# Half chunks in the first group, wide clock products, and a reordered end in a cross-network kernel

## The chip, the cores and the metric

The kernel runs on one core of a Trainium2 chip. The metric is the device time of the core in microseconds (us); lower is better. A run with 5 rounds gives five or six timed executions, set against executions of the kernel before on the same chip.

## The reference

Six layers of a cross network on 16,384 rows of 416 features, in bfloat16:

```python
B, F, D, L = 16384, 26, 16, 6          # Din = F * D = 416
def reference(x0, ws, bs):
    x = x0
    for l in range(6):
        proj = jnp.einsum('bd,de->be', x, ws[l]) + bs[l]
        x = x0 * proj + x
    return x
```

The kernel keeps x transposed (features on partitions) and cuts 416 features into three full tiles of 128 and a tail of 32. The rows are eight groups of 2048, each of four chunks of 512. Groups are worked in pairs, layer by layer: TensorE (PE) multiplies, ScalarE (ACT) adds the bias, VectorE (DVE) does `x0 * proj + x`. Group 0 is loaded in natural order and transposed by PE. All later groups are loaded by transposing DMAs. The last layer of the last group writes natural-order output directly, for which x itself (the "residual") must be transposed back by DMA.

## The kernel before

Loads, in the order of the SP queue:

```python
    def load_group(g, between=lambda: None):
        ...
        turn(0)                          # a transposing DMA: 2048 rows x 128 features
        add("sp", lambda h: h.dma_start_transpose(Tb, x0[rows, D - P:D]), ...)   # the tails
        turn(1)
        turn(2)
        between()
        for j in range(NJ):              # four small copies of the tails, after Tb has landed
            q = slice(j * T32, (j + 1) * T32)
            add("sp", lambda h, q=q, j=j: h.dma_start(x0s[s][q, XW:XW + CH], Tb[P - T32:P, j * CH:(j + 1) * CH]), ...)
    ...
    load_nat(0, 0, 2)
    load_nat(0, 2, KK)
    load_wm(0, "sp")
    for j in range(1, NJ):
        load_nat(j, 0, KK)               # chunks 1 to 3 of group 0, each whole
    load_w3(0, "sp")
    load_group(1, lambda: load_wm(1, "sp"))
```

The products that only keep the clock up ("clock products"), and the first job:

```python
    def keep_busy(n, b):
        for _ in range(n):
            add("pe", lambda h: h.matmul(bank(b, n=P), ones[:, :], ones[:, :], start=True, stop=True), ...)
    keep_busy(22, 7)

    def transposed_chunk(j):             # 16 transposes: tiles 0, 1, 2 and a fourth that holds the 32 tails
        first = (0, P, 2 * P, D - P)
        ...                              # then two ACT copies, a DVE copy, and a 32-row DVE copy of the tails

    def first_job():
        transposed_chunk(0)
        ...
        keep_busy(8, 3)
        full(g, l, 0, ba, True, True, chunks=[0])
        full(g, l, 1, bb, True, True, chunks=[0])
        transposed_chunk(1)
        transposed_chunk(2)
        full(g, l, 0, ba, True, True, chunks=[1])
        transposed_chunk(3)
        load_w3(1, "act")
        full(g, l, 1, bb, True, True, chunks=[1])
        full(g, l, 0, ba, True, True, chunks=[2, 3])
        ...
```

The end:

```python
    def rest_turn(t):                    # the residual, one transposing DMA per tile
        add("sp", lambda h: h.dma_start_transpose(
            x5f[:, :, t * P:(t + 1) * P], xs[s][:, t * GC:(t + 1) * GC]), ...)
    ...
    spread("act")                        # tails of group 6 into its output tile
    store(LAST - 1, 0, 2)                # group 6: two halves of 832 KB
    store(LAST - 1, 2, NJ)
    ...                                  # row block 0 of the last job
    for j in (0, 2):
        nat_mul(0, j)
        sums.append((0, j))
    nat_sum()                            # one sum; the other is carried into the next row block
    for kk in range(1, KK):
        ...                              # each block: two products and two sums, one sum late throughout
```

## Time and profile before

| | |
|---|---|
| time, three runs at the outset | 476.79 us (476.71 to 477.15) |
| span of the profiled execution | 475.7 us |
| first tail product of group 1 | 22.78 us |
| first product of the last job | 458.39 us |
| last PE product, last DVE sum, end of span | 470.78, 472.89, 475.69 us |

The three last rows are the marks to cut a trace into head, middle and end. The change touches nothing between the second and the third.

The first line covers 8 to 24 us (0.4 us a slice), the second 460 to 464 us (0.1 us a slice). The third is the page's own line on the queue that fetches instructions.

```profile
GB/s 256 126 103 130 23 20 180 291 290 224 108 152 102 10 164 289 287 308 219 206 215 251 249 292 179 243 288 289 288 228 264 354 175 119 67 18 0 0 0 146
GB/s 46 0 0 15 138 202 218 218 200 215 205 369 223 205 200 156 38 3 0 0 0 8 8 8 10 10 8 10 13 207 289 289 292 292 287 294 292 287 323 377
q8 instruction: 26, 0.43, 0.4%
```

A transposing load runs at 287 to 294 GB/s, and now and then nearly everything stops: near 10 and near 13.2 us in the first line, from about 461.7 to 462.9 in the second. The last two of these stops each follow the start of one instruction fetch of 16 KB (0.43 MB in 26 packets on that queue), which ran from 12.05 to 13.01 and from 461.19 to 462.14 us; near the stop at 10 us there is none.

### The profile page before, as it was taken

What the parts mean: (1) busy time and instruction counts of PE and PEld (TensorE: products, weight loads), DVE (VectorE), ACT (ScalarE), POOL (GpSimd) and SP (SyncE); (2) the same over time, 40 slices, a digit from 0 to 9 for tenths busy, and PEclk for the clock granted to TensorE, in tenths of its full rate; (3) what the DMA queues carried; (4) which work ended last, traced back from release to release, by engine and by line L of the source; (5) the groups of instructions that cost most, each with busy time, mean ns of one, the idle gap of its engine ahead of it and who ended that gap; (6) DMA issues with size and microseconds to landing.
All of it is one profiled execution on the core that took longest, in us unless ns stands there. A gap on an engine that the chain in (4) does not pass through costs nothing.

```text
span 475.7 us, 8355 instructions
## 1 busy us (share of the span) xinstructions
PE 462.2 (97%) x3325; PEld 195.7 (41%) x3379; DVE 404.0 (85%) x696; ACT 342.4 (72%) x372; POOL 6.8 (1%) x15
## 2 busy tenths in 40 slices
PE   7999999999999999999999999999999999999995
PEld 6344444444444444444444444434444444444442
DVE  2888888888888888898889869988888888888896
ACT  4677777777777777777777777777777777777785
POOL 1000000000000000000000000000000000000000
PEclk9999999999999999999999999999999999999999
DMA  8866950640002397369308940990000039025899
GB/s 223 181 150 137 190 113 1 142 81 1 28 7 44 63 228 158 76 139 244 84 21 195 208 108 9 178 279 2 1 10 25 4 64 242 15 45 117 227 155 288
DMA packets 138363, 53.31 MB, mean 112 GB/s; under 512 B 112330, under 2 KB 137428, under 8 KB 138324
## 3 DMA queue, kind: packets, MB, share of 16 engines
q1 hardware_dynamic: 137848, 52.46, 49.2%
q8 instruction: 26, 0.43, 0.4%
q10 hardware_dynamic: 476, 0.32, 0.2%
q14 instruction: 13, 0.11, 0.1%
HBM read 5.97 MB, written 13.63 MB: 41 GB/s over the span
## 4 chain that ended last, share of the span: by engine, by line
PE 95%; issue 1%; DMA 1%; ACT 1%; DVE 1%; SPq 0%
PE ps L456 77%; PE ps L477 7%; PE ps L497 6%; PE ps L798 2%; DMA x<-in_x_dram 1%; PE ps L471 1%; ACT tw L394 1%; PE ps L561 1%; PE ps L488 1%; DVE x L864 0%; PE ps L809 0%; ACT x L852 0%; DVE x L858 0%; PE ps L841 0%; SPq L521 0%
## 5 line engine op out<-in xcount | busy, mean ns | idle before, releaser
L394 ACT ACTIVATE tw<-ps,bias 128x1024 bf16<-128x1024 f32 (+1 forms) x295 | 299.8, 1071 | 119.8 <-PE ps L477 80.7
L456 PE MATMUL ps<-x,wm 128*128 128x512 bf16 x1638 | 371.7, 379 | 5.8 <-issue 3.7
L456 PEld LDWEIGHTS ps<-x,wm 128*128 128x128 bf16 x1692 | 158.9, 98 | 213.5 <-issue 27.9
L403 DVE TENSOR_TENSOR tw<-tw,x 128x1024 bf16<-128x1024 bf16 (+1 forms) x285 | 192.3, 682 | 52.8 <-ACT tw L394 52.4
L408 DVE TENSOR_TENSOR x<-tw,x 128x1024 bf16<-128x1024 bf16 (+1 forms) x285 | 183.0, 682 | 0.0
L477 PE MATMUL ps<-x,w 32*128 32x512 bf16 x512 | 39.2, 379 | 0.0
L497 PE MATMUL ps<-x,wm 128*32 128x512 bf16 x564 | 33.0, 380 | 0.0
L434 ACT ACTIVATE ts<-ps,bias 128x512 bf16<-128x512 f32 x47 | 28.8, 701 | 0.0
L438 DVE TENSOR_TENSOR x<-ts,x 128x512 bf16<-128x512 bf16 x47 | 18.6, 417 | 3.7 <-DMA x<-x 3.6
L497 PEld LDWEIGHTS ps<-x,wm 128*32 128x32 bf16 x564 | 13.8, 96 | 17.6 <-issue 5.3
L477 PEld LDWEIGHTS ps<-x,w 32*128 32x128 bf16 x512 | 7.8, 92 | 27.6 <-issue 27.1
L436 DVE TENSOR_TENSOR ts<-ts,x 128x512 bf16<-128x512 bf16 x47 | 18.5, 417 | 0.0
L666 POOL COPY ost<-ot 128x512 bf16<-128x512 bf16 x6 | 5.4, 898 | 423.7 <-DMA ot<-x 423.7
L798 PE MATMUL ps<-wm,x 128*128 128x416 bf16 x48 | 9.5, 340 | 0.0
L852 ACT ACTIVATE x<-ps 128x416 bf16<-128x416 f32 x16 | 7.7, 533 | 2.0 <-PE ps L798 1.9
L568 DVE COPY x<-ps 128x512 bf16<-128x512 bf16 x4 | 1.7, 424 | 8.7 <-PE ps L561 8.7
L565 ACT ACTIVATE x<-ps 128x512 bf16<-128x512 bf16 x8 | 4.3, 594 | 5.6 <-PE ps L561 5.6
L798 PEld LDWEIGHTS ps<-wm,x 128*128 128x128 bf16 x48 | 4.3, 98 | 4.2 <-issue 1.0
L561 PE MATMUL ps<-ident,x 128*128 128x128 bf16 x64 | 4.6, 226 | 1.4 <-DMA x<-in_x_dram 0.9
L858 DVE TENSOR_TENSOR x<-x,x 128x832 bf16<-128x832 bf16 (+1 forms) x10 | 5.0, 504 | 1.1 <-ACT x L852 1.1
L488 PE MATMUL ps<-x,w 32*32 32x512 bf16 x188 | 5.9, 374 | 0.0
L471 PE MATMUL ps<-x,w 32*32 32x512 bf16 x208 | 5.6, 385 | 0.0
(38 smaller groups left out, 35.7 us busy)
## 6 DMA issues: line engine op xcount, KB each, us to landing
out_dram<-ost SPq DMA_DIRECT2D x6, 1664.0 KB, 7.1
x<-in_x_dram SPq DMA_DIRECT2D x7, 416.0 KB, 8.0
x<-x SPq DMA_DIRECT2D x24, 96.0 KB, 2.2
wm<-in_ws_dram SPq DMA_DIRECT2D x6, 312.0 KB, 3.7
out_dram<-ost SPq DMA_DIRECT2D x2, 832.0 KB, 6.7
x<-x SPq DMA_DIRECT2D x22, 64.0 KB, 2.0
out_dram<-x SPq DMA_DIRECT2D x3, 416.0 KB, 3.6
x<-ost SPq DMA_DIRECT2D x28, 32.0 KB, 2.2
```

Of the source, the lines that this page charges most:

```text
L394: add("act", lambda h, a=a, w=w, b0=b0: h.activation(tw[r][:, a * CH:(a + w) * CH], psum[:, b0 * CH:(b0 + w) * CH], ACT_F.Identity, bias=b ...
L403: add("dve", lambda h, a=a, e=e: h.tensor_tensor(tw[r][:, a * CH:e * CH], tw[r][:, a * CH:e * CH], x0s[s0][:, i * GC + a * CH:i * GC + e * ...
L408: add("dve", lambda h, a=a, e=e: h.tensor_tensor(xs[so][:, i * GC + a * CH:i * GC + e * CH], tw[r][:, a * CH:e * CH], src(i, a, e), ALU.ad ...
L434: add("act", lambda h: h.activation(ts[r][:, :], bank(b), ACT_F.Identity, bias=bias[:, 3, l:l + 1], scale=1.0), reads=[("ps", b), "bias"], ...
L436: add("dve", lambda h: h.tensor_tensor(ts[r][:, :], ts[r][:, :], x03, ALU.mult), reads=[("ts", r)] + tok0, writes=[("ts", r)], release=True)
L438: add("dve", lambda h: h.tensor_tensor(x3s[so][:, :], ts[r][:, :], res, ALU.add), reads=[("ts", r)] + rtok, writes=[("x3", so), ("x3", so, ...
L456: add("pe", lambda h, t=t, j=j: h.matmul(bank(banks[j]), wm[l][:, t, ecols], src(t, j, j + 1), start=(first and t == 0), stop=(not first a ...
L471: add("pe", lambda h, q=q, j=j, r=r, c=c, o=o: h.matmul(psum[o, banks[j] * CH:(banks[j] + 1) * CH], w3[l][q, i * P + c * T32:i * P + (c + ...
L477: add("pe", lambda h, q=q, j=j, r=r: h.matmul(bank(banks[j]), w3[l][q, ecols], src[q, :], start=first, stop=not first, tile_position=(r * ...
L488: add("pe", lambda h, l=l, b=b, s3=s3, ri=ri, qi=qi, ro=ro, qo=qo: h.matmul(psum[qo, b * CH:(b + 1) * CH], w3[l][qi, NT * P:D], s3[qi, :], ...
L497: add("pe", lambda h, t=t, j=j, src=src, l=l, b=b, ro=ro, qo=qo: h.matmul(psum[qo, b * CH:(b + 1) * CH], wm[l][:, t, NT * P:D], src(t, j, ...
L798: add("pe", lambda h, t=t: h.matmul(bank(b, n=D), xcol(t, j, kk), wm[l][:, t, :], start=(first and t == 0), stop=(not first and t == NT - 1)),
```

## The change

It has five intents: PE is to begin on half chunks and transpose all 32-wide tails of group 0 together, in four column groups at once; the second weights are to give way to group 1's tail copies; the clock products are to need fewer instructions; the spread, a quarter store and a halved residual are to use DMA earlier at the end; and the sums are to run without their lag, the last store in two. Cut to its core:

```diff
-    def load_group(g, between=lambda: None):
+    def load_group(g):
         turn(1)
         turn(2)
-        between()
         for j in range(NJ):
             ...                                        # tail copies
+        if g == 1:
+            load_wm(1, "sp")
+            load_w3(1, "sp")
     for j in range(1, NJ):
-        load_nat(j, 0, KK)
+        load_nat(j, 0, 2)
+        load_nat(j, 2, KK)
     def keep_busy(n, b):
-        for _ in range(n):
-            add("pe", lambda h: h.matmul(bank(b, n=P), ones, ones, ...))
+        while n > 0:
+            m = min(n, 4)                               # one product of 512 columns for four of 128
+            add("pe", lambda h, m=m: h.matmul(bank(b, n=m * P)..., ones, ones....broadcast_to([P, m, P]), ...))
+            n -= m
     def transposed_chunk(j):
-        ...                                            # 16 transposes, chunk by chunk
+        for k2 in (0, 2):                              # 12 transposes, half by half
+            ...
+    def transposed_tails(b):                           # 16 transposes 32 wide, 4 column groups; one DVE copy
-        keep_busy(8, 3)
+        keep_busy(5, 3)
         full(g, l, 0, ba, True, True, chunks=[1])
+        full(g, l, 1, bb, True, True, chunks=[1])
         transposed_chunk(3)
-        load_w3(1, "act")
-        full(g, l, 1, bb, True, True, chunks=[1])
+        transposed_tails(7)
     def rest_turn(t):
-        add("sp", ... whole tile ...)
+        for j0, j1 in ((0, NJ),) if t == 0 else ((0, 2), (2, NJ)):
+            if t and j0:
+                store(LAST - 1, 0, 1)                   # a quarter, 416 KB, between the halves
+            add("sp", ... chunks j0 to j1 ...)
         if (g, l) == (LAST, L - 2) and i < NT - 1:
+            if i:
+                spread("act")
             rest_turn(i)
-    spread("act")
-    store(LAST - 1, 0, 2)
+    store(LAST - 1, 1, 2)
     store(LAST - 1, 2, NJ)
-    ...                                                # sums one behind
+    ...                                                # sums at once; last block: store of chunks 0-1, then 2, then 3
```

## The prediction

> **What bounds the kernel now.** I read the page first: busy time, then the chain that ended last.
>
> ```profile
> PE 462.2 (97%) x3325; PEld 195.7 (41%) x3379; DVE 404.0 (85%) x696; ACT 342.4 (72%) x372; POOL 6.8 (1%) x15
> ...
> PE 95%; issue 1%; DMA 1%; ACT 1%; DVE 1%; SPq 0%
> ```
>
> TensorE (PE) is busy 97% of 475.7 us and is 95% of the chain. The change touches none of the products between about 25 and 455 us, so it can only win (a) the us by which PE reaches its unbroken stretch earlier, (b) gaps at the hand-over to the last job, (c) what follows PE's last product. I therefore read the chain in order of time at both ends. Columns: start, duration, what.
>
> ```profile
> 2.13 5.75 DMA x<-in_x_dram
> 7.88 0.05 issue
> 7.92 1.08 PE ps L561 x16
> 9.01 0.02 issue
> 9.03 0.43 DVE x L568
> 9.46 0.10 issue
> 9.56 1.05 PE ps L561 x16
> 10.61 0.65 PE ps L456 x3
> 11.26 0.89 PE ps L561 x16
> 12.15 0.05 issue
> 12.21 1.89 PE ps L456 x8
> ```
>
> Chunk 1 of the first group lands at 7.88, PE transposes it (L561), waits for a copy, transposes chunk 2, and so on; the last products of chunks 1 to 3 end at 14.10. From there PE runs without a real gap. The chain names the copy at L568 before chunk 2, but the landing records of the trace have chunk 2 landing at 9.42, nearly together with that copy's end (9.45): both held it. Of chunk 1, 15 of 16 landing parts were there by 6.51 and the last at 7.88; for chunk 2 it is 7.55 and 9.42. One lagging part decides.
>
> The end, same columns, then three lines of the timeline (start, duration, engine, line, count, idle before it):
>
> ```profile
> 470.31 0.38 DVE x L858
> 470.69 1.01 DVE x L864 x2
> 471.69 0.58 DVE x L858 x2
> 472.27 0.02 issue
> 472.30 0.59 DVE x L864
> ```
> ```profile
> 454.98 4.59 ACT L394 ACTIVATE tw<-ps,bias 128x512 bf16<-128x512 f32 x7 [0.21 <-PE ps L456]
> ...
> 459.41 0.67 ACT L664 ACTIVATE ost<-ot 128x512 bf16<-128x512 bf16 x1
> ...
> 459.97 0.27 PE L827 MATMUL ps<-ident,x 32*128 32x32 bf16 x16
> ...
> 464.49 0.59 DVE L864 TENSOR_TENSOR x<-x,x 128x832 bf16<-128x832 bf16 x1 [0.32 <-DMA x<-x]
> ```
>
> VectorE (DVE) has two sums back to back at 470.69: one is a sum held over from the row block before (the lag). ScalarE (ACT) is gapless from 454.98 to 460.08; the spread of group 6's tails (L664) is its last piece. The last store is issued at 472.92 and lands at 475.2.
>
> **What the Trainium skill says.** (1) "DMA: Bandwidth & Descriptors", section "Why a DMA increments its semaphore by 16 and not by 1": only the full 16 means that all data has landed. The trace agrees: the 7.88 above is the 16th part. Halving a load does not remove a lagging part, it only lets half the data be counted earlier. (2) Same page, "Queues, rings and completion order": each DMA engine consumes descriptors in ring order. So what is put ahead on the SP queue delays what is behind; the second transposed half will queue behind the quarter store. (3) "TensorE: Matmul & The Clock Gate", Part 3: small products in different 32-column groups run concurrently. The trace agrees on the 32-wide tail products: 12 of L497 took 0.76 us of the chain, where 12 full ones take 2.7. (4) Same page, Part 1: the clock is released by some 3.4 us of activity, not by a count. Here transposes go from 105 to 56 ns apart at about 4.0 us, 3.0 us after the first product.
>
> **The change part by part.**
>
> *Wide clock products.* 22 products of 128 columns took 2.53 us (0.115 each, slow clock). 6 wide ones stream the same 2816 columns: about the same time. Later 2 become 1 of the same columns, and 8 become 5 columns' worth of 128. They lie ahead of data that PE waits for (PE idles 0.87 us before 7.92). Worth 0.
>
> *Half chunks, and tails apart.* Each of four chunks loses its 4 fourth-column transposes: 16 at 56 ns is 0.9 us of PE, of which the 12 in chunks 1 to 3 (0.67) lie on the path. Added are 16 narrow ones in 4 concurrent column groups, about 4 x 0.06 to 0.3 us, and one 128x512 copy (0.42 on DVE) in place of four 32-row copies (0.43 each). Reckoned forward: chunk 2's second half lands at about 9.45 (same bytes, same lagging part; its first half was transposed before, in the time in which PE now waits). Six transposes: 9.85. Six products of chunk 1 at 0.216: 11.15. Chunk 3, 12 transposes: 11.82. Tails: 12.15. Six products of chunks 2 and 3: 13.45, plus about 0.1 because bank 7 is read by the tail copy first. Before: 14.10. Gain 0.55, say **0.6**.
>
> *Does the next group follow?* The SP queue gets three more load issues of 0.43, so 1.3 us later for the transposing loads of group 1. But their first one sat in issue from 6.44 to 10.56, because transposing packets stood still until the lagging part was through at 10.4; most of the 1.3 falls into that. Second weights now come behind the tail copies and off the ACT queue.
>
> ```profile
> 18.02 0.59 SPq L280 DMA_DIRECT2D wm<-in_ws_dram x1
> ...
> 18.66 2.52 SPq L304 DMA_DIRECT2D x<-ost x4
> ...
> 22.77 0.12 PEld L477 LDWEIGHTS ps<-x,w 32*128 32x128 bf16 x8 [0.42 <-DMA x<-ost]
> ```
>
> The four tail copies landed at 22.53, just ahead of their use at 22.78. Moving the 0.6 us weight issue behind them lets them land near 21.9 plus any delay of the transposes; the earlier PE wants them at 22.1 to 22.2. That fits with up to 0.2 of delay: this reordering is what lets the 0.6 through. The second weights then are issued near 20.5 and land 3.1 to 3.8 later, about 24.3; they are wanted at 25.9 less 0.6. Also hidden. I take 0.1 off: head **-0.5**.
>
> *Spread before the last tile's evictions.* The spread's source landed at 457.16, and ACT ends the tile before at 457.25: no wait, but the 0.67 us now stands ahead of the last four evictions, which end at 460.24 instead of 459.56. The tail transposes (L827, at 459.97) need those banks, so they move to about 460.3, and the copy behind them (L834) and PE's next transposes (460.97) with it. Cost **+0.3**, less if PE has other slack.
>
> *Quarter store between transposed halves.* The residual's first half can be issued at 458.7 (its tile is done at 458.58, SP free at 458.73) instead of 459.21. The quarter store, 416 KB at the 330 to 375 GB/s that this stretch shows, puts 1.2 us ahead of the second half, which then lands near 464.4, as now. DMA idles from 461.5 to 463 in the trace, so stores start about 1.5 us sooner, but none of them ends the program. Worth 0 by itself; it lets sums start without the lag.
>
> *Sums unlagged, last store split.* After the last ACT piece (471.33) DVE still has, before: two products and one wide sum, ending at 472.89. After: without the held-over wide sum, product 1 ends 470.69, sum 0-1 471.24, products 2 and 3 471.9, two narrow sums at about 0.34 each: 472.55. Gain 0.34. The last stores carry 104 KB instead of 208 KB: at 350 GB/s 0.3 us less, of which I count half. Together **-0.5**.
>
> Sum: -0.5 + 0.3 - 0.5 = -0.7; with the head's uncertainty leaning to a gain I take -0.8: 476.79 - 0.8 = **476.0 us**.
>
> **Rivals.** *Group 1 becomes the wait.* If the three extra issues delay the transposed loads by the full 1.3 us, tail copies land at 23.2 and PE waits 1.1 us: the head loses 0.4 instead of gaining, and the time is near 477. For: the copies now land only 0.25 us ahead. Against: the stand-still up to 10.4, and the weights taken out of the way. *The lagging part moves.* It may not lag with twice as many, smaller packets; then chunk 2 lands near 7.6 and the head gains until group 1 binds, 0.9 us at most: 475.5. *The residual's second half lands late* (behind the store, after 465.3): DVE has only 0.3 us of slack for each row block of 2.67 us, so unlagged sums would carry the delay to the end and eat the 0.34: 476.4. *The spread costs nothing* if L827's place has more slack than I see: 475.7.
>
> **Range and chances.** The parts are each under 1 us and 2% is 9.5 us, so only a failure outside this list leaves the band. Runs of the kernel before spread over 0.44 us. The rivals span 475.5 to 477; 8 in 10 from 475.2 to 476.8. Faster by over 2%: 0.01; within 2%: 0.98; slower: 0.01.
>
> **What would show it.** Head: transposes of chunk 1 start before 7.9 in two runs of six; products of chunks 2 and 3 end near 13.5; no wait of PE at the tail copies' first use. Tail: the spread starts near 457.3 (less the shift), the last eviction ends 0.7 later, L827's counterpart waits for ACT. End: the last sum ends about 1.2 us after ACT's last piece (1.56 now) and two narrow stores land last. It would be wrong if PE idles near 20 to 23 us, if the second half lands after 465, or if the middle of the run, which I take as unchanged, moves.

## More of the kernel before

The profiled execution itself took 477.49 us, more than any of the timed ones, so its trace is that of a rather slow run.

## The result, and the profile after

The changed kernel took **477.06 us** (476.52 to 477.91, six runs). The kernel before took 477.02 (476.71 to 477.37, six runs) in the same rounds. The ratio is 1.0003, with a 95% interval of 0.9990 to 1.0016: the same. A ratio is the mean time of one kernel's fast runs over that of the other's of the same rounds, so it is not quite the ratio of the two medians. The predicted 476.0 was about 1 us too low, and the result is 0.26 us outside the range.

The trace of the changed kernel is that of its slowest execution, 477.91 us. Runs e3 and e5 below have the same head and clock products, and their traces come to group 1's first tail product 1.2 us sooner. So what this trace loses there is not what the kernel always loses. From its page, the busy times and the shares of its chain (the work and waits that ended last, followed back from the last instruction):

```profile
PE 467.7 (98%) x3356; PEld 193.4 (41%) x3356; DVE 403.3 (85%) x695; ACT 341.7 (72%) x371; POOL 5.8 (1%) x15
PE 90%; SPq 4%; DVE 3%; DMA 2%; ACT 0%; issue 0%; DVEq 0%
```

The counts of matmul records mislead, since some were missing before (3325 products against 3379 weight loads). The weight loads tell it: 3379 became 3356, 23 fewer. With 23 fewer products that is 46 fewer PE instructions. And in the chain PE has lost 5% of the span to the SP queue, DMA and DVE.

**The head.** The PE timeline of the changed kernel from the last products of group 0's chunks on (start, duration, engine, line, operation, shapes, count, idle before and what ended it; L478, before the change L477, is the line of kernel.py with the tail products); then its chain of waits up to the first tail product of group 1:

```profile
12.31 0.40 PE L478 MATMUL ps<-x,w 32*128 32x512 bf16 x4
...
21.08 1.04 PE L457 MATMUL ps<-x,wm 128*128 128x512 bf16 x4 [0.82 <-DMA x<-in_x_dram]
22.89 0.61 PE L478 MATMUL ps<-x,w 32*128 32x512 bf16 x8 [0.77 <-DMA x<-ost]
```
```profile
6.89 3.68 SPq L292
...
10.62 2.12 SPq L297
...
12.78 3.60 SPq L292
...
16.43 2.57 SPq L292
...
20.96 1.88 DMA x<-ost
22.84 0.05 issue
22.89 0.61 PE ps L478 x8
```

The same two views of the kernel before from the same mark on:

```profile
14.03 0.40 PE L477 MATMUL ps<-x,w 32*128 32x512 bf16 x4
...
20.31 2.54 PE L456 MATMUL ps<-x,wm 128*128 128x512 bf16 x11 [0.16 <-issue]
22.78 0.61 PE L477 MATMUL ps<-x,w 32*128 32x512 bf16 x8
```

PE does reach the mark 1.7 us sooner (12.31 for 14.03), and then, in this trace, gives all of it back in two waits, 0.82 us for group 1's third transposed tile and 0.77 us for its tail copies. Group 1's first tail product starts at 22.89 us, where it was 22.78. The chain of the changed head is no longer PE's: it runs through the SP queue's transposing loads (L292, L297), one after the other.

**The end.** The chain of the changed kernel, and the DVE timeline at the wait:

```profile
460.91 5.35 DMA x<-x
466.26 0.03 issue
...
466.38 0.59 DVE x L887
...
473.25 0.29 DVE x L887
473.54 0.28 DVEq L174
```
```profile
464.54 0.59 DVE L887 TENSOR_TENSOR x<-x,x 128x832 bf16<-128x832 bf16 x1
466.38 0.59 DVE L887 TENSOR_TENSOR x<-x,x 128x832 bf16<-128x832 bf16 x1 [1.25 <-DMA x<-x]
```

The second half of the residual lands at 466.26 us. DVE waits for it 1.25 us, and from there the chain never leaves DVE again until its last sum. The DMA view of the changed kernel from 463 to 467 us, 0.1 us a slice, and its queue lines, show what happened meanwhile:

```profile
GB/s 220 207 223 223 218 172 195 225 205 386 302 225 0 0 0 0 0 0 3 8 8 10 8 10 10 11 42 391 374 374 374 349 308 341 300 374 316 342 291 366
q8 instruction: 1, 0.02, 1.5%
```

From 464.2 to 465.6 us next to nothing moves, and just before, at 463.95 us, PE began to fetch instructions (until 464.90). That the one causes the other is only suggested here; e5 tests it. The Trainium skill, "Runtime: NRT & Kernel Launch", section "Instruction fetch mechanics", states that an engine's instructions come in blocks of 16 KiB, 256 instructions, over a DMA queue of its own, and that crossing a block is mostly hidden. The trace agrees on the size (26 fetches for some 6,700 PE instructions) and on PE itself, which does not stall (its 12 products from 463.59 us on take 2.28 us). But the transposing load in flight stands still. The fetch at the end was at 461.19 us before and is at 463.95 now, the one in the head was at 12.05 and is at 14.11. The 46 instructions that the wide clock products save have a part in this: where they alone change (e10), the two move to 464.57 and 13.38 us.

### The profile page after: what moved, and what is told of

Its sections match the earlier page's. It is cut to its first block, busy times and chain, and to the rows that moved or that the text cites. A ratio compares the mean times of both kernels' runs of the same rounds, so it can differ in the third digit from the quotient of the medians.

```text
span 476.1 us, 8364 instructions
## 1 busy us (share of the span) xinstructions
PE 467.7 (98%) x3356; PEld 193.4 (41%) x3356; DVE 403.3 (85%) x695; ACT 341.7 (72%) x371; POOL 5.8 (1%) x15
## 4 chain that ended last, share of the span: by engine, by line
PE 90%; SPq 4%; DVE 3%; DMA 2%; ACT 0%; issue 0%; DVEq 0%
PE ps L457 75%; PE ps L478 7%; PE ps L498 7%; SPq L292 2%; DMA x<-x 1%; PE ps L472 1%; DVE x L887 1%; SPq L522 1%; DVE x L881 1%; DVE x L409 1%; DVE tw L404 1%; PE ps L489 1%; SPq L297 0%; ACT tw L395 0%; DMA x<-ost 0%; SPq L303 0%
## 5 line engine op out<-in xcount | busy, mean ns | idle before, releaser
L457 PE MATMUL ps<-x,wm 128*128 128x512 bf16 x1692 | 379.6, 380 | 1.3 <-DMA x<-in_x_dram 0.8
L478 PE MATMUL ps<-x,w 32*128 32x512 bf16 x512 | 39.2, 379 | 0.8 <-DMA x<-ost 0.8
L478 PEld LDWEIGHTS ps<-x,w 32*128 32x128 bf16 x512 | 7.8, 92 | 28.5 <-issue 27.1
L684 POOL COPY ost<-ot 128x512 bf16<-128x512 bf16 x6 | 4.3, 720 | 423.7 <-DMA ot<-x 423.7
L887 DVE TENSOR_TENSOR x<-x,x 128x832 bf16<-128x832 bf16 (+1 forms) x9 | 4.8, 542 | 1.4 <-DMA x<-x 1.3
L881 DVE TENSOR_TENSOR x<-x,x 128x832 bf16<-128x832 bf16 (+1 forms) x10 | 4.8, 500 | 0.7 <-ACT x L875 0.7
```

The source lines that it names most:

```text
L457: add("pe", lambda h, t=t, j=j: h.matmul(bank(banks[j]), wm[l][:, t, ecols], src(t, j, j + 1), start=(first and t == 0), stop=(not first a ...
L478: add("pe", lambda h, q=q, j=j, r=r: h.matmul(bank(banks[j]), w3[l][q, ecols], src[q, :], start=first, stop=not first, tile_position=(r * ...
```

## The experiments

The marks of every profiled run, in us. "Tail" is group 1's first tail product, "last job" the first product of the last job. The next three columns split the end: from "last job" to PE's last product, from there to DVE's last sum, from there to the end of the span. "Residual" is when its last part landed, counted from "last job". "Fetch" gives the starts of the PE instruction fetches in head and end.

```
                    tail  last job   PE    DVE   store  end   residual   fetch
before             22.78   458.39  12.39  2.11  2.80  17.30    5.98    12.1, 461.2
after              22.89   458.50  12.73  2.59  2.29  17.60    7.76    14.1, 463.9
e1_head            21.59   457.20  12.39  2.10  2.80  17.28    6.02    11.1, 460.0
e2_tail            21.95   457.56  12.56  2.54  2.24  17.34    7.53    10.8, 460.6
e3_whole_rest      21.73   457.34  12.73  1.68  3.19  17.60    5.69    13.8, 462.4
e4_fetch_on        23.38   459.08  12.70  2.79  2.27  17.77    7.92    16.3, 465.0
e5_fetch_end       21.64   457.65  12.71  1.67  2.89  17.27    6.14    12.4, 467.5
e6_plain_group1    21.22   456.83  12.73  2.62  2.28  17.62    7.79    14.9, 462.4
e7_late_spread     23.01   458.63  12.38  1.68  3.52  17.59    5.68    14.3, 463.7
e8_w3_on_act       21.63   457.25  12.72  2.61  2.27  17.60    7.76    13.7, 462.7
e9_narrow_order    22.76   458.37  12.38  1.93  3.01  17.32    6.24    12.1, 461.2
e10_clock_alone    23.90   459.51  12.39  2.11  3.09  17.59    5.69    13.4, 464.6
e11_narrow         22.52   458.13  12.72  2.38  2.28  17.38    7.54    11.4, 462.6
e12_head_w3_act    21.73   457.35  12.39  2.11  2.89  17.38    6.37    10.9, 460.2
```

From "tail" to "last job" it is 435.6 or 435.7 us in every trace but e5 (436.0): the middle did not move, as predicted. The end repeats to 0.1 us where code and landings repeat. The head does not: each row is one execution. Where effects are below 1 us the ratio of the timed runs decides, and the trace only says where to look.

The theory at the outset was that group 1 takes over the head and the moved fetch spoils the end. Its rivals were that one of the five parts simply costs more than reckoned, or that the SP queue's extra issues, not the loads themselves, hold group 1 up. All runs had 5 rounds.

**e1: the head alone.** The kernel before with the new head, narrow clock products and the old end.

```diff
  # after, but
-        keep_busy(5, 3)      # and the wide keep_busy
+        keep_busy(8, 3)      # and the narrow one
-            if i: spread("act")
-        # halves, quarter store, unlagged sums
+        # rest_turn, stores and sums of before
```

> The kernel before with the change's head alone (half chunks, tails apart, second weights behind the tail copies), the clock products narrow, so that TensorE has as many instructions as before; the end is the old one. Theory (group 1's arrival takes the head's gain): TensorE ends the first job's chunk products near 12.4 us instead of 14.1, then idles near group 1's third transposed load and the tail copies, and meets the tail rows of group 1 at 22.5 to 23.2 us: within 0.4 us of the kernel before. Rival (the head's gain gets through and only the end gave it back): 0.5 to 1.7 us faster.

Measured: 476.45 us, ratio 0.9990 (0.9978 to 1.0002), that is -0.5 us with 0 at the edge of the interval. The predicted head was -0.5. So the theory missed and the rival came true, at its lower edge: in this trace group 1's first tail product starts at 21.59 us, before the 22.5 to 23.2 that the theory asked for.

**e2: the end alone.** The kernel before with the new end; old head, narrow clock products.

```diff
  # before, but
+            if i: spread("act")
+        # halves, quarter store, unlagged sums, last store split
```

> The kernel before with the change's end alone (spread early, residual in two transposes with the quarter store between, sums unlagged, last store split), head as before. Theory (residual's second half lands late and the unlagged sums carry the wait to the end): second half lands at 465.5 us or later, a DVE wait of 0.7 us or more, 0.3 to 1 us slower than before. Rival (the end is a gain of its own, as predicted): 0.2 us faster or better, second half near 464.4.

Measured: 476.99 us, ratio 0.9997 (0.9984 to 1.0010), that is -0.1 us; the predicted end was -0.2. The theory is half right: the second half lands late (7.53 us after the last job's first product) and DVE ends 2.54 us after PE, but the time is not 0.3 to 1 us longer. Its head is the old one, yet in this trace group 1's first tail product starts at 21.95 us, 0.8 us before the 22.78 of the one trace that I predicted from. So the old head's chunk products, which ended at 14.10 in that trace, do not always end so late (13.26 here, by the chain; the timeline's mark is 13.20):

```profile
13.20 0.40 PE L477 MATMUL ps<-x,w 32*128 32x512 bf16 x4
...
21.95 0.61 PE L477 MATMUL ps<-x,w 32*128 32x512 bf16 x8
```

**e3: the residual whole again**, in the changed kernel, no quarter store ahead of it.

```diff
-        for j0, j1 in ((0, NJ),) if t == 0 else ((0, 2), (2, NJ)):
+        # one transposing DMA per tile
-    store(LAST - 1, 1, 2)
+    store(LAST - 1, 0, 2)
```

> The changed kernel with the residual's transpose whole again and no quarter store ahead of its second half; spread early, sums unlagged, last store split stay. Theory: the whole residual lands near 462.5 to 463.5, before the 16 KB instruction fetch at about 464, DVE no longer waits, time 0.6 to 1.1 us below the changed kernel. Rival (the end is set by ScalarE and the spread, not by the residual): within 0.2 us of the changed kernel.

Measured: 476.74 us, ratio 0.9993 (0.9981 to 1.0005). The residual now lands 5.69 us after the last job's first product and DVE ends 1.68 us after PE, against 2.59: the late half was what held the sums. But the end as a whole is still 17.60. What DVE won, the stores took back (3.19 for 2.29): the store that no longer went ahead is now in the queue before the last ones. That is my reading; no run tests it. The time fell short of the expected 0.6 to 1.1 us: by the ratios it is 0.5 below the changed kernel, inside the noise.

**e4: the fetch moved on.** One more tile of the changed kernel with four wide products in place of the narrow ones: 24 PE instructions fewer, the same work.

```diff
+    wide4 = [n for n in sorted(mode) if mode[n] == "F1"][-1:]
-            rows32(g, l, i, banks, False, mode[n] == "F1")
+            rows32(g, l, i, banks, False, mode[n] == "F1" and n not in wide4)
```

> The changed kernel, but the last of the tiles that take their 32 rows in 16 narrow products takes them in 4 wide ones: 24 TensorE instructions fewer before the end, so the 16 KB instruction fetch now seen at 463.95 us comes some 2 us later, near 465.7; nothing else changes. Theory (the fetch freezes the transposing queue and with it the second half's landing): second half lands near 464.4, time 0.6 to 1.1 us below the changed kernel. Rival (the half is late because the quarter store stands ahead of it): it still lands near 466, same time as the changed kernel.

A miss. Measured: 477.36 us, ratio 1.0012 (0.9996 to 1.0027). The fetch moved only to 464.98 us, still inside the residual's flight. Fifteen of the 16 parts of the second half landed by 465.47, that is 6.39 us after the last job's first product, the last one only at 467.0. Two of the six timed runs stand apart (478.65 and 479.02). The profiled one shows another kind of bad head: the clock was released only at 10.01 us. These are the six first products of this run and of the changed kernel, PE timeline:

```profile
6.38 2.72 PE L457 MATMUL ps<-x,wm 128*128 128x512 bf16 x6 [0.37 <-ACT bias L608]
```
```profile
5.82 1.46 PE L457 MATMUL ps<-x,wm 128*128 128x512 bf16 x6 [0.46 <-DMA wm<-in_ws_dram]
```

The products take twice as long before the release. In all other traces the clock was released between 3.84 and 6.19 us. One trace does not say whether the wide clock products make such a miss likelier.

**e5: the fetch moved past the residual.** As e4, with the last four such tiles (96 instructions fewer).

```diff
+    wide4 = [n for n in sorted(mode) if mode[n] == "F1"][-4:]
```

> The changed kernel with the last four of the tiles that take their 32 rows in 16 narrow products taking them in 4 wide ones: 96 TensorE instructions fewer before the end, so the last 16 KB instruction fetch (5.1 to 5.9 us after the last job's first product so far) falls at the end of TensorE's work or is gone, and the one before it moves by the same count to about 450 us. Theory (the fetch is what makes the residual's second half, or the last stores, late): second half lands under 6.3 us after the last job's first product (7.5 to 7.9 so far), that product to the end of the program 16.6 to 17.0 us instead of 17.6, time 0.6 to 0.9 us below the changed kernel. Rival (the queue's order alone makes the half late): 7.5 us or more again and the same end. If the earlier fetch hurts group 6's transposes, the last job starts later by up to 1 us and the sum is a wash.

Half right. Measured: 477.23 us, ratio 0.9993 (0.9972 to 1.0014). With the fetch at 467.5 us, the second half landed at 6.14 instead of 7.76 us, and DVE ended 1.67 us after PE. The parts, the quarter store and the order are those of the changed kernel; only the fetch is elsewhere. The half was issued 2.41 us after that product in both traces. Its DMA view from 461 to 465 us, 0.1 us a slice, has no stop:

```profile
GB/s 333 324 250 241 349 391 349 349 250 201 189 223 230 215 225 212 195 192 200 228 232 289 340 383 383 349 333 216 275 341 366 366 391 341 366 333 374 358 316 374
```

So the fetch is what made the half late. All six traces in which a fetch met the second half have it at 7.5 us or later. The end missed its expectation (17.27 for 16.6 to 17.0): the fetch now fell among the final stores, whose piece took 2.89 us. The time is 0.5 us below the changed kernel's by the ratios, inside the noise.

**e6: group 1 by plain loads.** The changed kernel with the four transposing loads of group 1 replaced by plain ones of the same bytes. Its output is wrong, which doesn't matter for the time.

```diff
-            add("sp", lambda h: h.dma_start_transpose(
-                x0s[s][:, t * GC:(t + 1) * GC], x0[rows, t * P:(t + 1) * P]), ...)
+            add("sp", lambda h: h.dma_start(x0s[s][:, t * GC:(t + 1) * GC], flat[:, t * GC:(t + 1) * GC]) if g == 1
+                else h.dma_start_transpose(...), ...)
```

> The changed kernel with group 1 loaded by plain copies of as many bytes in place of transposing ones: group 1's result is wrong on purpose. Theory (the head's gain waits for group 1): TensorE no longer idles at group 1's third tile and tail rows, meets the tail rows near 21.3 us or before (22.9 in the changed kernel's trace, 21.7 in the better ones), time 0.8 to 1.6 us below the changed kernel. Rival (TensorE's own work bounds the head): within 0.3 us.

Measured: 476.33 us, ratio 0.9970 (0.9954 to 0.9987). That is 1.4 us under the kernel before, and some 1.6 us under the changed kernel's 1.0003; those two intervals don't meet. Its PE timeline:

```profile
12.47 0.39 PE L480 MATMUL ps<-x,w 32*128 32x512 bf16 x4
...
21.22 0.61 PE L480 MATMUL ps<-x,w 32*128 32x512 bf16 x8
```

There is no wait for DMA left, and 8.75 us lie between the marks where the changed kernel needs 10.58. The end is unchanged (17.62). So the transposing loads of group 1 hold back part of what PE's new head would have gained. The 1.6 us is the largest estimate of that part. Against e5, e7 and e8, which have this head (e8 but for one weight queue) and ran in the same rounds, it is 0.6 to 0.9 us by the medians. And 8.75 us is PE's own time between the marks: it is also what the kernel before needs, and e2, e8 and e12. Beyond it, the nine traces with the new head, transposing loads and a clock in time lose between 0 (e8, e12) and 1.83 us (the changed kernel), 0.6 in the mean.

**e7: the spread late again**, the residual whole, sums unlagged and last store split as in the change.

```diff
-            if i: spread("act")
+    spread("act")            # before the stores, as before
+    # rest_turn and stores of before
```

> The changed kernel with the old order of spread, residual and group 6 stores, but the unlagged sums and the split last store kept. Theory (spread ahead of the last evictions costs TensorE 0.34 us): first product of the last job to TensorE's last falls from 12.73 to 12.39 us, 0.3 us below the run with the whole residual and early spread, or 0.3 to 0.6 below the changed kernel. Rival (the spread's place is free): same as the run with the whole residual.

Measured: 477.18 us, ratio 0.9990 (0.9973 to 1.0007). From the last job's first product to PE's last it is 12.38 us, against 12.73: the early spread costs 0.35. The end is 17.59 all the same, since its stores take 3.52 us.

**e8: the first tail weights on the ACT queue**, in the changed kernel, so that SP comes 1.7 us sooner to group 1.

```diff
-    load_w3(0, "sp")
+    load_w3(0, "act")
```

> The changed kernel with the four small weight loads of the first layer issued on ScalarE's queue, so the transposing loads of group 1 are issued 1.8 us sooner (near 5.0 instead of 6.9 us). Rival, as the prediction had it (three more issues on the SP queue delay group 1): group 1's tail copies land 1 to 1.8 us sooner, 0.7 us or more faster than the changed kernel. Theory (transposing packets stand still while the plain loads run and during instruction fetches, whenever they are issued): they land at most 0.5 us sooner, within 0.4 us.

Measured: 476.92 us, ratio 0.9982 (0.9966 to 0.9998). By the letter the rival came true: against the changed kernel's trace the tail copies landed 1.3 us sooner (21.55 for 22.84), and by the ratios the time is 1.0 us lower, although those two intervals overlap. But good heads that keep these weights on SP have their copies as soon (21.54 in e1, 21.59 in e5, 21.68 in e3). The first transposing load was issued at 5.17 us instead of 6.89, stayed in issue until 9.63, and did not bring the data sooner than there. PE did not wait for group 1 at all in this trace (8.75 us between the marks), so the SP queue did not bind it.

**e9: e7 with narrow clock products**, which puts the fetches back to 12.05 and 461.17 us.

```diff
-        keep_busy(5, 3)      # and the wide keep_busy
+        keep_busy(8, 3)      # and the narrow one
```

> The run with the late spread, whole residual, unlagged sums and split last store, but with the clock products narrow again: 46 TensorE instructions more in the first 6 us, nothing else. Theory (the count of TensorE's instructions sets where the last 16 KB instruction fetch falls, and there it is paid): fetch back to 2.8 to 3.1 us after the last job's first product (5.0 in the wide run), the residual lands near 6.0 us after it as in the kernel before, no lagging last part of the final stores; that product to the end of the program 16.5 to 16.9 us instead of 17.59, and 0.5 to 1 us below the kernel before. Rival (the fetch has no part in it): the end stays at 17.4 or more.

The fetch came where it was expected, the end did not: 17.32 us, not 16.5 to 16.9. Measured: 477.18 us, ratio 0.9991 (0.9978 to 1.0004). Its DMA view from 456 to 476 us, 0.5 us a slice:

```profile
GB/s 283 108 74 216 193 168 207 186 42 216 236 34 3 10 231 289 371 376 373 344 325 341 328 333 333 330 331 334 321 339 329 336 323 333 328 330 82 5 0 0
```

Once the stop at the fetch is over (the 34, 3 and 10 near 462) DMA runs at 320 to 376 GB/s from 464 until 474 us. From the residual's landing on, the stores alone fill the queue. My reading is that the end has three limits within some tenths of one another, PE, DVE's sums and the stores, and that easing one hands the end to the next.

**e10: the wide clock products alone**, in the kernel before.

```diff
-        for _ in range(n):   # n products of 128 columns
+        while n > 0:         # products of up to 512 columns
-        keep_busy(8, 3)
+        keep_busy(5, 3)
```

> The kernel before with the wide clock products alone (and 5 columns' worth instead of 8 of the last ones): 46 TensorE instructions fewer, all in the first 6 us. Theory: the last fetch moves from 2.8 to 5 us or more after the last job's first product, falls on the group 6 stores and leaves one part of every later store behind: last DVE sum to the end of the program 3.1 us or more instead of 2.80, end 17.6 to 18.2 us instead of 17.3, 0.3 to 0.8 us slower. Rival (as predicted, worth 0): end 17.3 us, same time.

Measured: 478.50 us, ratio **1.0022** (1.0008 to 1.0035): this part, which I had put at 0, costs 1.05 us (0.4 to 1.7) in the kernel before. The expectation looked for the loss in the end; most of it shows in the head. The DMA view from 8 to 24 us and the PE timeline:

```profile
GB/s 235 268 226 147 158 67 198 291 291 206 68 108 108 276 201 8 5 9 182 289 316 226 196 244 291 291 142 92 111 198 273 291 288 329 262 346 131 82 0 0
```
```profile
23.90 0.40 PE L477 MATMUL ps<-x,w 32*128 32x512 bf16 x4 [0.77 <-DMA x<-ost]
```

The fetch has moved from 12.05 to 13.38 us, into the second and third transposing loads, and three slices (14.0 to 15.2) stand at 5 to 9 GB/s where the kernel before had one after its fetch. Group 1's tail copies land at 23.85 us instead of 22.53, and PE, which did not wait for them before, waits 0.77 us. The end is 0.3 us longer, in its stores. The time is measured; that the moved fetch is its cause rests on this one trace, as the edit also changes what PE does while its clock comes up (released at 6.04 us here, 3.84 before).

**e11: the changed kernel with narrow clock products.**

```diff
-        keep_busy(5, 3)      # and the wide keep_busy
+        keep_busy(8, 3)      # and the narrow one
```

> The changed kernel with the clock products narrow again. Theory: as in the run with the changed end on the old head, the fetch falls between the residual's two halves and the second lands 7.5 us after the last job's first product; end 17.3 to 17.4 us; the head as in the run with the head alone. Within 0.4 us of the changed kernel, with no gain from the end. Rival (only the wide products spoil the end): second half under 6.5, end 16.8 or less, 0.7 us below the changed kernel.

Measured: 477.32 us, ratio 0.9997 (0.9985 to 1.0009). Against the changed kernel's 1.0003 that is 0.3 us, inside both intervals. And e7 and e9, which differ by the clock products alone, have the same ratio (0.9990 and 0.9991). So the 1.05 us of e10 did not come back when the clock products were taken out of the whole change. The end came as expected, the head did not (22.52 us, not e1's 21.59). The fetch at the end came to 462.6 us and froze the second half there too (7.54 us).

**e12: the new head with the first tail weights on the ACT queue**, narrow clock products, old end: it puts together what had helped.

```diff
  # e1, but
-    load_w3(0, "sp")
+    load_w3(0, "act")
```

> The kernel before with the new head alone (narrow clock products, old end), and the tail weights of layer 0 issued on the ACT queue instead of the SP queue. It is the version put together from what helped, and a second trace of e1's head. Theory (the transposing loads of group 1 themselves bind the head, not the SP queue's issues): group 1's tail rows start at 21.5 to 21.7 us as in e1 if no freeze beyond about 10 us hits the first transposing load, at 22.5 to 23 if one does; end 17.3 from the last job's first product (12.39 + 2.1 + 2.8), the fetch near 460; time ratio to the kernel before 0.998 to 0.9995. Rival (SP issue binds, so freeing the queue brings group 1 sooner than in e1): tail rows start before 21.3 us and the ratio is below 0.9975.

Measured: 476.51 us, ratio 0.9992 (0.9976 to 1.0009). Of the correct kernels this one, e8 and e1 have medians 0.5 to 0.7 us under that of the kernel before on their chip, and only e8's interval leaves out 1, by a hair. No version here can be called faster by more than that. The tail copies landed at 20.99 us, 0.55 sooner than in e1: this trace has no standstill in the head, and there the earlier issue may have helped. PE came no sooner for it:

```profile
18.02 0.32 PE ps L489 x4
18.34 0.76 PE ps L498 x12
19.10 2.70 PE ps L457 x12
21.80 0.54 PE ps L478 x8
```

Here the chain runs through PE without a gap: what ended late was group 0's own chunks (the mark at 12.98 us, not 12.31).

## Why the prediction was wrong

**What held.** PE's unbroken middle did not move. The spread's "Cost +0.3" measured 0.35 (12.73 against 12.38; in e2, with the old head, 0.17). PE's own part of the new head gains what was reckoned or more: the products of chunks 2 and 3 were to end at 13.45, and the mark behind them stands between 12.31 and 13.47 us in ten traces whose clock came up in time, against 13.20, 14.03 and 14.32 in the three of the old head. And two sums held when measured apart, though neither interval excludes 0: head -0.5 (e1: -0.5), end -0.2 (e2: -0.1). Both are partly luck. The end's sum holds although its largest term did not (below). The head's rested on a lagging part that halving would not remove, with chunk 2's second half at about 9.45 us. In the eleven traces with halves it landed between 8.06 and 9.25 us, in the changed kernel at 8.08 with its last part 0.19 after the 15th. With whole chunks, chunk 2 landed at 9.42, 8.04 (e2) and 9.36 (e10). So the lag comes and goes from run to run, and the second rival, "*The lagging part moves*", was nearer.

**First failed step: "Wide clock products... Worth 0."** I asked only whether their columns lie on PE's path, and they don't. What I left out: 46 PE instructions fewer move the later instruction fetches. The one in the head starts at 10.8 to 12.1 us in the six traces with narrow clock products and at 12.4 to 14.9 in the seven with wide ones and a clock in time. And a fetch that meets transposing loads can stop them, for 0.5 to 1.4 us in the views shown; not every one does (e12's at 10.87 us stopped nothing). I had not looked at the instruction queue at all, since it is 0.4% of the DMA time. A count over all fourteen traces bears this out: of 53 standstills of 0.8 us or longer (slices of 0.1 us under 26 GB/s, with ten or more packets in flight) 52 begin within 1.5 us after the start of a fetch, while only 12% of the time lies so near to one, and these 52 end 0.7 to 0.9 us after the fetch itself has ended. What the moved fetches cost in time is less clear: 1.05 us in the kernel before (e10), but 0.3 (changed kernel against e11) and 0.0 (e7 against e9) inside the change, which is within the noise.

**Second: "That fits with up to 0.2 of delay: this reordering is what lets the 0.6 through."** The copies were to land near 21.9 us and PE to want them at 22.1 to 22.2. But PE's new head is ready for them sooner than reckoned, at 21.1 to 22.2 (the mark plus 8.75), and the copies come when the transposing loads ahead of them let them: at 22.84 in the changed kernel's trace and 22.47 to 22.96 in e7, e9 and e11, at 20.99 to 21.68 in the five other traces with a clock in time. So the gain gets through in some executions and not in others. This was my rival "Group 1 becomes the wait", with its mechanism partly wrong: it blamed three extra issues for 1.3 us, but the first transposing load was issued only 0.45 us later (6.89 for 6.44), and the loads themselves stand still twice (about 9.2 to 10.4, and 14.4 to 15.6 after the start of the fetch). The DMA view of the changed kernel from 8 to 24 us shows both:

```profile
GB/s 255 209 183 16 35 10 159 292 289 216 52 177 225 278 250 248 3 3 9 118 286 281 291 289 187 90 136 212 290 291 261 85 82 10 72 72 10 77 220 374
```

e6 shows that these loads hold the head back: without transposing loads the same kernel is 0.6 to 1.6 us faster, by what it is set against.

**Third: the quarter store is "Worth 0 by itself", its second half "then lands near 464.4".** It landed at 466.26. Store and order were reckoned right: with the fetch elsewhere (e5) it lands 6.14 us after the last job's first product, which in the changed kernel's trace is 464.64. The other 1.6 us are the fetch. The wide clock products are not needed for this: with narrow ones a fetch met the second half too (7.53 us in e2, 7.54 in e11). Where the residual stays whole, it lands 5.98 to 6.37 us after that product with the fetch in mid-flight (2.8 us, the kernel before, e1, e9 and e12) and at 5.68 or 5.69 with the fetch near its end (5.1 us, e3, e7 and e10): there the fetch costs only 0.3 to 0.7 us. That the half queues behind the quarter store fits the landings (463.54, then 466.26 us), though no run takes that store alone away. With the late half my third rival came true as well. The unlagged sums have no slack for a late half: where it lands by 6.2 us, DVE ends 1.67 to 1.93 us after PE; where it lands at 7.5 or later, 2.38 to 2.79; with the lag it was 2.10 or 2.11, for landings from 5.7 to 6.4. So **"Gain 0.34"** became a loss of 0.48 (2.59 against 2.11). In the trace it was paid back by the stretch after the last sum, where the **half of 0.3** that I counted was 0.51 (2.80 to 2.29). The split last store alone does not explain that: with the same split but earlier sums the stretch is 2.89 to 3.52 (e3, e5, e7, e9). The end that I had at -0.2 came out at +0.30 in the trace: 17.60 against 17.30, to rounding the sum of +0.34, +0.48 and -0.51.

**A fault of method.** I reckoned everything forward from one trace. Its head (22.78) was a poor one for the old code, as e2's 21.95 shows, so part of the gain was a gain over an accident. And with runs of one kernel up to 1.4 us apart (476.52 to 477.91), a range of 1.6 us was too narrow around a sum of small terms.

**What stays open.** How the missing microsecond divides between clock products, head and end is not settled: the parts measured apart (e1 -0.5, e2 -0.1) and the whole with narrow clock products (e11, -0.1) differ by less than their intervals, and e10's 1.05 us does not agree with the 0.3 and 0.0 inside the change. The standstill at about 9.2 to 10.4 us, which the traces before and after both have, holds no fetch, and its cause was not found. The prediction laid it to the lagging part, but the changed kernel has it without one. Nor does it alone tell good heads from poor ones: e7 and e11 come to the first tail product at 23.01 and 22.52 us without a full stop there. Nor was a fetch moved by itself in the head; only at the end (e4, e5).

## What to carry to other kernels

Before you change the number of instructions on an engine, even in dead time, look where its instruction fetches fall, and keep them away from transposing DMAs that something waits for. When a stage's engine is made faster, set the landing of what it will want next against the new time, from the loads' own duration and not from their place in the queue. And for effects below 1 us take several traces of the kernel before as the base: a single one can be a poor run of the stage in question.

## What the Trainium skill lacked or had wrong

- "Runtime: NRT & Kernel Launch", section "Instruction fetch mechanics", calls the cost of a 16 KiB block mostly hidden. It is for PE, but the page lacks what it does to DMA: in the changed kernel transposing DMA stood at 0 to 11 GB/s from 464.2 to 465.6 us, and moving the fetch (e5) brought the second half of the residual 1.6 us sooner. Over fourteen traces 52 of 53 long standstills follow a fetch.
- "DMA: Bandwidth & Descriptors", section "Latency and other measured facts", gives 261 GB/s as the effective rate of a transposing DMA with a non-contiguous middle dimension, and some 350 to 400 for the contiguous case; no run here tells which case these loads are. Here they ran at 287 to 294 GB/s between standstills, and with them group 1's four loads (2.10 MB, from the first issue at 6.89 to the last landing at 21.04 us in the changed kernel) came to 148 GB/s.
- "TensorE: Matmul & The Clock Gate", Part 1, gives some 3.4 us of activity to the release. With PE working from 0.99 us on, the release came between 3.84 and 6.19 us in thirteen traces and at 10.01 us in one (e4). The page calls the count of slow products variable and advises not to fit to it; but beside a warning of a monitor stuck at a quarter of the clock it has no case of a release 5.75 us behind that of nearly the same code (4.26 us in the changed kernel).
- No page that I found says that a standstill of the transposing DMA can also come without any fetch, as from about 9.2 to 10.4 us in the changed kernel.
